# Batch 1's convolution cut by columns instead of by stream, and round 1's side work moved a tile or two

## The chip, the cores and the metric

The kernel runs on one core of one Trainium2 chip. The metric is the device time of one execution in microseconds (us), smaller is better. The profile is of one execution; its span runs from the first to the last instruction of the program on that core. Engines are named as in the profile: PE is TensorE, ACT is ScalarE, DVE is VectorE, POOL is GpSimd, SP is SyncE, which here only issues DMAs.

## The reference

A causal convolution with softmaxed taps per head, then a feed-forward block whose two last matrices follow each other without anything between them:

```python
# x: (8, 3904, 192), weight: (8 heads, 7 taps), group = 192 // 8 = 24 columns per head
w = softmax(weight, axis=-1)
out = einsum('hk,bskhg->bshg', w, windows of 7 rows of zero-padded x)
x = out.reshape(31232, 192)
a, b = x @ w1, x @ w2              # w1, w2: 192 x 1024
h = a * b @ w3                     # w3: 1024 x 1024
return h @ w_out                   # w_out: 1024 x 192
```

## The kernel before, in words

The 31232 tokens are two streams of 15616 (NS = 2): r = 0 is the first half, r = 1 the second. Both go through the kernel side by side in rounds of 512 tokens. `first_product(R)` makes round R's a * b: for each of eight feature tiles ft of 128 it fills a PSUM tile pa (for w1) and a PSUM tile pb (for w2) by six matmuls each, both streams in each; ACT casts pa into asb (line 603), DVE multiplies asb by pb into abT (line 605). `second_product` (line 621) multiplies abT by W_sb, which is w3 @ w_out, made by the kernel itself during the first rounds: `w3_turn` transposes a part of w3 on DVE (line 682), `w3_product` multiplies it by w_out. A dictionary handed to `first_product` names what is issued behind a tile: `{4: f}` calls f when the product of ft 4 has been issued. So the order on each engine is the order in which the program is written out; there is no planner, and each engine works through its queue in that order.

All PSUM tiles (pa, pb, cps, tps, wps, ops) come from one pool of four, handed out in turn: a new tile waits until the reader of the tile four before it is done.

The tokens are convolved in batches of windows of 32 rows, of which 26 come out as results. Batches 0, 1 and 2 have 20 windows per stream, some 520 tokens, one for each of the rounds 0, 1 and 2. POOL issues the loads of x into the tile xb, one per stream for batches 1 and 2 (line 158), stream 0 on partitions 0 to 31, stream 1 on partitions 64 to 95. The convolution is a set of matmuls with 32 x 32 weights (Aband) from xb into a PSUM tile cps; casts bring cps into the tile convo (in bf16, in three blocks k of 64 columns, each with both streams). There are two forms of it:

- `conv(b, c0, wd, evict)` (line 328) takes wd columns from c0 of both streams, 32 matmuls for 96 columns, r innermost. Its casts (line 337, or line 234 where the cast goes through `AV`) follow `segments(c0, wd)`: columns 0 to 95 are 64 columns of block 0 and then 32 of block 1; columns 96 to 191 are 32 of block 1 and then 64 of block 2. With `AV` a segment of 64 columns is cast by ACT and one of 32 by DVE; without `evict` all casts are ACT's.
- `conv_stream(b, r)` (line 357) takes all 192 columns of stream r, also 32 matmuls, two of its casts on ACT and two on DVE (line 364), in that order.

When a batch is in convo, `pe_transposes(b)` (line 401) turns it on PE, 15 transposes into a tile tps, block by block, and copies on ACT (block 0) and DVE (blocks 1 and 2) bring it into xT (line 408), from where the next round's first_product reads it. `store(2, ...)` lets SP write the rows of batch 2 that later rounds need to memory (line 392); `load_taps` then sends the taps through SP (lines 434 and 439).

Where the work around the change stands before: behind round 0's ft 4 and ft 5 the two streams of batch 1, behind ft 6 its transposes; behind round 1's ft 2 and ft 3 the two units of batch 2, behind ft 3 also w3_turn(0), behind ft 5 its transposes and its store.

Of the kernel before, what the change touches and what calls it, by code (L numbers as in the profile page):

```python
# [9 lines left out]
BF16 = mybir.dt.bfloat16  # L10
# [6 lines left out]
def kernel(  # L17
# [10 lines left out]
    nc = tc.nc  # L28

    B, S, D = x.shape  # L30
    H, K = weight.shape
    G = D // H
# [4 lines left out]
    NS = 2  # L37
    TS = B * S // NS
    CH = 512
# [4 lines left out]
    Q = 64  # L44
    NP = D // Q
    C = 32
    ST = C - PAD
    LAG_ROWS = (LAG + 1) * CH
# [43 lines left out]
    work = ctx.enter_context(tc.tile_pool(name="work", bufs=2))  # L92
# [4 lines left out]
    def banks(name):  # L97
        return psum.tile([128, NS, CH], FP32, tag="banks", name=name)
# [13 lines left out]
    def shape_of(b):  # L112
        n = SIZES[b] // 4
        m = n // (1 if b < 3 else 2)
        return n, m, n // m
# [4 lines left out]
    xb_of, zero_rows = {}, {}  # L120

    def group(r, e):
        return slice((2 * r + e) * C, (2 * r + e) * C + C)
# [57 lines left out]
    for r in range(NS):  # L181
        p = group(r, 0).start
# [12 lines left out]
        out=diag, in_=diag, pattern=[[-1, 128 + 8]], compare_op=ALU.is_equal,  # L195
# [11 lines left out]
    for i in range(4):  # L207
        d = diag[i * C:i * C + C, i * C + 2 * i:i * C + 2 * i + C]
        nc.vector.tensor_copy(
            out=cmask[i * C:i * C + C],  # L210
            in_=bass.AP(tensor=d.tensor, offset=d.offset, ap=[d.ap[0], [1, 2], [1, C]]))
# [10 lines left out]
    V, A, P = nc.vector.tensor_copy, nc.scalar.copy, nc.gpsimd.tensor_copy  # L222
# [33 lines left out]
    for i in range(3):  # L256
# [3 lines left out]
        out=share[:, :, 0:K], in0=taps.unsqueeze(1).to_broadcast([H, H, K]), scalar=total,  # L260
        in1=diag[0:H, 0:H].unsqueeze(2).to_broadcast([H, H, K]), op0=ALU.mult, op1=ALU.mult)
    spread = banks("spread")
    for i in range(4):
# [6 lines left out]
        out=wsb, in_=spread[:, 0, 0:2 * H].rearrange("p (h k) -> p h k", h=H)  # L270
# [5 lines left out]
        out=cprod.rearrange("p h k (s two) -> p h k s two", two=2),  # L276
# [6 lines left out]
    p = group(1, 0).start  # L283
    nc.vector.memset(xb_of[0][0][0][p:p + PAD, 0, :], 0.0)
    Aband = const.tile([128, H, C], BF16)
    bps = banks("bps")
    for k in range(2):
# [3 lines left out]
            start=(k == 0), stop=(k == 1))  # L291
    nc.vector.tensor_copy(out=Aband,
                          in_=bps[:, 0, 0:C * H].rearrange("p (h s) -> p h s", s=C))
# [5 lines left out]
    convo_of, left_of = {}, {}  # L299
    wt = {}  # L300

    def segments(c0, n):
        out = []
        while n:
            m = min(n, Q - c0 % Q)
            out.append((c0 // Q, c0 % Q, m))
            c0, n = c0 + m, n - m
        return out

    def conv(b, c0, wd, evict=(nc.scalar.copy,), es=None):  # L310
        n, m, E = shape_of(b)
        es = range(E) if es is None else es
        if b not in convo_of:
            convo_of[b] = work.tile([128, n, NP, NS, Q], BF16, tag="convo", bufs=2,
                                    name="convo")
            left_of[b] = D * E
        convo = convo_of[b]
        cps = {e: banks("cps") for e in es}
        c = c0
        while c < c0 + wd:  # L320
            h = c // G
            c1 = min(h * G + G, c0 + wd)
            for j in range(4):
                xb, s = xb_of[b][j]
                for e in es:
                    for r in range(NS):
                        o = cps[e][j * C:j * C + C, r, 0:m * wd]
                        nc.tensor.matmul(  # L328
                            o.rearrange("p (w g) -> p w g", g=wd)[:, :, c - c0:c1 - c0],
                            Aband[group(r, e), h, :], xb[group(r, e), s:s + m, c:c1],  # L330
                            start=True, stop=True)
            c = c1
        for f, e in zip(evict, es):
            src = cps[e][:, :, 0:m * wd].rearrange("p r (w g) -> p r w g", g=wd)
            o = 0
            for k, lo, c in segments(c0, wd):
                f(out=convo[:, e::E, k, :, lo:lo + c]  # L337
                    .rearrange("p w r g -> p r w g"), in_=src[:, :, :, o:o + c])
                o += c
        left_of[b] -= wd * len(es)  # L340
        if not left_of[b]:
            del xb_of[b]

    def conv_stream(b, r):
        n, m, E = shape_of(b)
        assert E == 1 and 2 * m * D // 2 <= 2 * CH
        if b not in convo_of:
            convo_of[b] = work.tile([128, n, NP, NS, Q], BF16, tag="convo", bufs=2,
                                    name="convo")
            left_of[b] = NS  # L350
        convo = convo_of[b]
        cps, wd = banks("cps"), D // 2
        for h in range(H):
            o = h * G % wd
            for j in range(4):
                xb, s = xb_of[b][j]
                nc.tensor.matmul(  # L357
                    cps[j * C:j * C + C, h * G // wd, 0:m * wd]
                        .rearrange("p (w g) -> p w g", g=wd)[:, :, o:o + G],
                    Aband[group(r, 0), h, :], xb[group(r, 0), s:s + m, h * G:h * G + G],  # L360
                    start=True, stop=True)
        for a, k, lo, o, c, f in ((0, 0, 0, 0, Q, A), (1, 2, 0, C, Q, A),
                                  (0, 1, 0, Q, C, V), (1, 1, C, 0, C, V)):
            f(out=convo[:, :, k, r, lo:lo + c],
              in_=cps[:, a, 0:m * wd].rearrange("p (w g) -> p w g", g=wd)[:, :, o:o + c])
        left_of[b] -= 1
        if not left_of[b]:
            del xb_of[b]

# [211 lines left out]
    def first_product(R, between=None):  # L581
        N = width(R)
        ab = work.tile([128, JT, NS, CH], BF16, tag="abT", bufs=LAG + 1, name="abT")
        abT_of[R] = ab
        per = CH // N if CH % N == 0 else 1
        for f0 in range(0, JT, per):
            pq = []
            for i in range(2):
                p = banks("pa" if i == 0 else "pb")
                pq.append(p)  # L590
                for f in range(per):
                    ft = f0 + f
                    for k in range(NP):
                        for r in range(NS):
                            rs = slice(Q * r, Q * r + Q)
                            nc.tensor.matmul(  # L596
                                p[:, r, f * N:f * N + N],
                                w_of(i, k, r)[rs, ft * 128:(ft + 1) * 128],
                                operand(R, k, rs),
                                start=(k == 0), stop=(k == NP - 1))  # L600
            pa, pb = pq
            asb = work.tile([128, NS, CH], BF16, tag="asb", bufs=3, name="asb")
            nc.scalar.copy(out=asb[:, :, 0:per * N], in_=pa[:, :, 0:per * N])  # L603
            if per == 1:
                nc.vector.tensor_tensor(out=ab[:, f0, :, 0:N], in0=asb[:, :, 0:N],  # L605
                                        in1=pb[:, :, 0:N], op=ALU.mult)
            else:
                i0, i1 = (t.rearrange("p r (f n) -> p r f n", f=per) for t in (asb, pb))
                nc.vector.tensor_tensor(
                    out=ab[:, f0:f0 + per, :, 0:N].rearrange("p f r n -> p r f n"),  # L610
                    in0=i0, in1=i1, op=ALU.mult)
            if between and f0 in between:
                between[f0]()
# [87 lines left out]
    for i in range(4):  # L701
        conv(0, i * 2 * G, 2 * G, evict=((A, V)[i % 2],))
# [33 lines left out]
    starts, chain, begun, room, p = {}, {}, set(), 0, -1  # L736
    for i, cost, f in steps:
# [5 lines left out]
        if i not in begun:  # L743
            begun.add(i)
            starts[p].append(i)
            n = max(p == 0, int(at) // 2 - 1, -(-ends.get(i - 2, 0) // 2))
# [22 lines left out]
    def seq(*fs):  # L769
        def run():  # L770
            for f, *a in fs:
                f(*a)
        return run

    def later_loads():
# [12 lines left out]

    first_product(0, {
        2: later_loads,  # L790
        4: seq((conv_stream, 1, 0)),
        5: seq((conv_stream, 1, 1)),
        6: seq((pe_transposes, 1))})
    first_product(1, {
        2: seq((conv, 2, 0, 96, (AV,))),
        3: seq((conv, 2, 96, 96), (w3_turn, 0)),
        5: seq((pe_transposes, 2), (store, 2, LAG_ROWS // ST))})
    first_product(2, {
        1: seq((load_taps,), (w3_turn, 2)),
        3: seq((w3_product, 0), (w3_product, 2), (w3_turn, 4), (w3_turn, 6),  # L800
# [13 lines left out]
    for p, b, part, n in ((1, 5, 0, 0), (1, 5, 1, 4), (3, 6, 0, 0), (4, 6, 1, 0)):  # L814
        todo = x_jobs(b, part)
        n = n or len(todo)
# [129 lines left out]
```

## Time and profile before

| what | value |
|---|---|
| time, median of 3 runs (lowest to highest) | 511.17 us (510.73 to 512.86) |
| the profiled execution's own time | 510.92 us |
| its span | 509.2 us |
| PE busy | 503.8 us, 99% |
| DVE busy | 446.4 us, 88% |
| ACT busy | 347.2 us, 68% |
| POOL busy | 229.3 us, 45% |

The busy share of PE counts matmuls whose ends are modelled, so it says when PE has work, not how well it is used. Lines are those of the kernel before. A row of the timeline gives start, duration, engine, line, operation, output and input, shape and count; in brackets stands how long the engine was idle just before, and what ended that. In a row with a count above one the duration reaches from the first start to the last end.

### The profile page before, as it was taken

How to read it: one execution, taken by the hardware profiler on the slowest of the kernel's cores; microseconds unless marked ns; L12 is line 12 of the kernel's file. 1: busy time of each engine (PE TensorE's matmuls, PEld its weight loads, DVE VectorE, ACT ScalarE, POOL GpSimd, SP SyncE). 2: the span in 40 equal slices, each digit the busy share in tenths (PEclk: the TensorE clock that was granted, in tenths of full speed). 3: DMA queues.
4: the chain of work that ended last, by engine and by line, in shares of the span. 5: the costliest groups of instructions: out<-in, count | busy, mean ns of one | idle time of the engine just before them, and what ended most of it. 6: DMA issues, size and time to landing. Idle time of an engine off the chain costs nothing.

```text
span 509.2 us, 13681 instructions
## 1 busy us (share of the span) xinstructions
PE 503.8 (99%) x5758; PEld 338.5 (66%) x5758; DVE 446.4 (88%) x402; ACT 347.2 (68%) x386; POOL 229.3 (45%) x303
## 2 busy tenths in 40 slices
PE   8999999999999999999999999999999999999997
PEld 4546864595569557845875596569557855965597
DVE  7898769999999799899989999999899999999930
ACT  6786667836778776477667767763776477457752
POOL 9966101333980597079519902970573067100000
PEclk9999999999999999999999999999999999999999
DMA  9999979999955999963889337975501400230024
GB/s 136 158 162 174 173 152 177 148 163 194 159 60 159 143 158 133 229 79 23 65 219 96 24 106 127 192 110 155 102 1 43 156 4 0 84 106 1 1 63 156
DMA packets 156825, 58.45 MB, mean 115 GB/s; under 512 B 112607, under 2 KB 156763, under 8 KB 156763
## 3 DMA queue, kind: packets, MB, share of 16 engines
q0 software_dynamic: 70560, 16.85, 37.2%
q1 hardware_dynamic: 86043, 40.62, 36.1%
q8 instruction: 45, 0.74, 0.6%
q14 instruction: 17, 0.14, 0.1%
q10 hardware_dynamic: 160, 0.10, 0.1%
HBM read 33.97 MB, written 34.85 MB: 135 GB/s over the span
## 4 chain that ended last, share of the span: by engine, by line
PE 98%; DMA 1%; ACT 0%; POOL 0%; DVE 0%; issue 0%; POOLq 0%
PE ops L621 32%; PE pa L596 31%; PE pb L596 31%; PE cps L328 1%; PE wps L693 1%; DMA xb<-in_x_dram 1%; PE tps L401 0%; PE ops L646 0%; PE tps L416 0%; DVE abT L605 0%; PE cps L357 0%; ACT asb L603 0%; POOL xb L158 0%; ACT convo L337 0%; ACT osb L650 0%
## 5 line engine op out<-in xcount | busy, mean ns | idle before, releaser
L605 DVE TENSOR_TENSOR abT<-asb,pb 128x1024 bf16<-128x1024 bf16 x240 | 292.7, 1221 | 30.4 <-ACT asb L603 14.5
L603 ACT CAST asb<-pa 128x1024 bf16<-128x1024 f32 x244 | 247.0, 1012 | 64.2 <-PE pa L596 64.0
L596 PEld LDWEIGHTS <-wn 64*128 64x128 bf16 x1488 | 138.5, 94 | 79.7 <-issue 1.6
L596 PEld LDWEIGHTS <-ws 64*128 64x128 bf16 x1488 | 129.7, 94 | 70.0 <-issue 1.4
L621 PE MATMUL ops<-W_sb,abT 128*128 128x192 bf16 x1936 | 163.7, 246 | 0.0
L621 PEld LDWEIGHTS <-abT 128*128 128x128 bf16 x1936 | 158.5, 98 | 6.4 <-issue 6.4
L596 PE MATMUL pb<-xT,wn 64*128 64x512 bf16 x408 | 111.2, 376 | 0.0
L596 PE MATMUL pa<-xT,wn 64*128 64x512 bf16 x408 | 110.1, 376 | 0.1
L596 PE MATMUL pa<-xT,ws 64*128 64x512 bf16 x408 | 110.1, 376 | 0.0
L596 PE MATMUL pb<-xT,ws 64*128 64x512 bf16 x408 | 108.5, 376 | 0.0
L626 ACT COPY osb<-ops 128x768 f32<-128x768 f32 (+1 forms) x61 | 48.5, 795 | 84.7 <-PE ops L621 82.3
L876 POOL COPY pace<-abT 1x2 bf16<-1x2 bf16 x57 | 10.9, 192 | 175.5 <-DVE abT L605 155.0
L596 PE MATMUL pb<-side,wn 64*128 64x512 bf16 (+1 forms) x336 | 88.8, 368 | 0.0
L596 PE MATMUL pa<-side,ws 64*128 64x512 bf16 (+1 forms) x336 | 87.3, 369 | 0.0
L596 PE MATMUL pa<-side,wn 64*128 64x512 bf16 (+1 forms) x336 | 87.3, 369 | 0.0
L512 DVE SCALAR_TENSOR_TENSOR acc<-raw,wC,acc 128x1024 f32<-128x1024 bf16 (+2 forms) x70 | 84.6, 1209 | 2.0
L596 PE MATMUL pb<-side,ws 64*128 64x512 bf16 (+1 forms) x336 | 85.7, 368 | 0.0
L539 POOL TENSOR_SCALAR tmp<-acc,wC 128x512 f32<-128x512 bf16 x42 | 65.8, 1566 | 1.2
L559 POOL TENSOR_TENSOR acc<-acc,tmp 128x512 f32<-128x512 f32 x35 | 44.4, 1267 | 2.9
L480 POOL DMA_DIRECT2D rows_c<-in_x_dram x50 | 37.1, 744 | 4.7 <-issue 2.7
L158 POOL DMA_DIRECT2D xb<-in_x_dram x50 | 32.2, 649 | 6.9 <-DMA xb<-in_x_dram 2.2
L512 DVE SCALAR_TENSOR_TENSOR acc<-side,wC,acc 128x1024 f32<-128x1024 bf16 (+1 forms) x20 | 24.3, 1217 | 3.8 <-ACT acc L494 3.2
(76 smaller groups left out, 186.9 us busy)
## 6 DMA issues: line engine op xcount, KB each, us to landing
out_dram<-osb SPq DMA_DIRECT2D x54, 384.0 KB
xb<-in_x_dram POOLq DMA_DIRECT2D x16, 240.0 KB, 7.2
out_dram<-osb SPq DMA_DIRECT2D x12, 192.0 KB
rows_c<-in_x_dram POOLq DMA_DIRECT2D x16, 130.0 KB, 5.6
rows_c<-in_x_dram POOLq DMA_DIRECT2D x12, 128.0 KB, 5.7
rows<-convo SPq DMA_DIRECT2D x6, 240.0 KB
xb<-in_x_dram POOLq DMA_DIRECT2D x6, 228.0 KB, 4.9
w3b<-in_moe_w_dram POOLq DMA_DIRECT2D x4, 256.0 KB, 5.5
```

Source lines behind the costliest of these rows:

```text
L158: nc.gpsimd.dma_start(out=tiles[js[0]][0][group(r, e), s:s + w, :], in_=bass.AP(tensor=x.tensor, offset=(r * TS + t - PAD) * D, ap=[[D, C] ...
L328: nc.tensor.matmul(o.rearrange("p (w g) -> p w g", g=wd)[:, :, c - c0:c1 - c0], Aband[group(r, e), h, :], xb[group(r, e), s:s + m, c:c1], ...
L480: nc.gpsimd.dma_start(out=rows_c[lo:t1, k, r * Q:r * Q + Q], in_=x_rows[r * TS + lo:r * TS + t1, k * Q:k * Q + Q])
L512: nc.vector.scalar_tensor_tensor(out=side_of[p][:, k, o:o + t1 - t0] if last else a, in0=raw[:, HALO + lo - t0 - d:HALO + hi - t0 - d], sc ...
L539: nc.gpsimd.tensor_scalar(out=out, in0=pool_raw[0][:, HALO - d:HALO - d + CH], scalar1=wC[:, k, K - 1 - d:K - d], scalar2=None, op0=ALU.mult)
L559: nc.gpsimd.tensor_tensor(out=a, in0=a, in1=tmp[:, lo - t0:hi - t0], op=ALU.add)
L596: nc.tensor.matmul(p[:, r, f * N:f * N + N], w_of(i, k, r)[rs, ft * 128:(ft + 1) * 128], operand(R, k, rs), start=(k == 0), stop=(k == NP ...
L603: nc.scalar.copy(out=asb[:, :, 0:per * N], in_=pa[:, :, 0:per * N])
L605: nc.vector.tensor_tensor(out=ab[:, f0, :, 0:N], in0=asb[:, :, 0:N], in1=pb[:, :, 0:N], op=ALU.mult)
L621: nc.tensor.matmul(ops[:, g // 2, (g % 2) * D:(g % 2) * D + D], ab[:, jt, r, g * 128:(g + 1) * 128], W_sb[:, jt, :], start=(jt == 0), stop ...
L626: nc.scalar.copy(out=osb.rearrange("p (a g) d -> p a (g d)", g=2), in_=ops[:, 0:ng // 2, 0:2 * D])
L876: P(out=pace, in_=abT_of[R][0:1, ft, 1, 0:2])
```

## The change

`conv_stream` is gone. Batch 1 is convolved by `conv` in two units of 96 columns of both streams, at the same two places, with `AV` for the casts. The first unit of batch 2 is issued behind batch 1's transposes (round 0, ft 6) instead of behind round 1's ft 2; its second unit behind round 1's ft 1 instead of ft 3, and with `AV` instead of ACT alone; w3_turn(0) stays behind ft 3; batch 2's transposes and store go from ft 5 to ft 4. In the changed file every line below `conv` has a number 26 lower.

```diff
-    def conv_stream(b, r):
...
-        for a, k, lo, o, c, f in ((0, 0, 0, 0, Q, A), (1, 2, 0, C, Q, A),
-                                  (0, 1, 0, Q, C, V), (1, 1, C, 0, C, V)):
-            f(out=convo[:, :, k, r, lo:lo + c],
-              in_=cps[:, a, 0:m * wd].rearrange("p (w g) -> p w g", g=wd)[:, :, o:o + c])
...
     first_product(0, {
         2: later_loads,
-        4: seq((conv_stream, 1, 0)),
-        5: seq((conv_stream, 1, 1)),
-        6: seq((pe_transposes, 1))})
+        4: seq((conv, 1, 0, 96, (AV,))),
+        5: seq((conv, 1, 96, 96, (AV,))),
+        6: seq((pe_transposes, 1), (conv, 2, 0, 96, (AV,)))})
     first_product(1, {
-        2: seq((conv, 2, 0, 96, (AV,))),
-        3: seq((conv, 2, 96, 96), (w3_turn, 0)),
-        5: seq((pe_transposes, 2), (store, 2, LAG_ROWS // ST))})
+        1: seq((conv, 2, 96, 96, (AV,))),
+        3: seq((w3_turn, 0)),
+        4: seq((pe_transposes, 2), (store, 2, LAG_ROWS // ST))})
```

More of the change, by code (lines that the diff above doesn't have):

```diff
@@ L340, in conv @@
         left_of[b] -= wd * len(es)
-        if not left_of[b]:
-            del xb_of[b]
-    def conv_stream(b, r):
[L345 to L361, printed above, removed]
-        for a, k, lo, o, c, f in ((0, 0, 0, 0, Q, A), (1, 2, 0, C, Q, A),
-                                  (0, 1, 0, Q, C, V), (1, 1, C, 0, C, V)):
-            f(out=convo[:, :, k, r, lo:lo + c],
-              in_=cps[:, a, 0:m * wd].rearrange("p (w g) -> p w g", g=wd)[:, :, o:o + c])
-        left_of[b] -= 1
         if not left_of[b]:
```

## The prediction

> **What bounds the kernel now.** I read the page first: busy shares, granted clock and the chain that ended last.
>
> ```profile
> span 509.2 us, 13681 instructions
> PE 503.8 (99%) x5758; PEld 338.5 (66%) x5758; DVE 446.4 (88%) x402; ACT 347.2 (68%) x386; POOL 229.3 (45%) x303
> PEclk9999999999999999999999999999999999999999
> PE 98%; DMA 1%; ACT 0%; POOL 0%; DVE 0%; issue 0%; POOLq 0%
> ```
>
> PE is the chain: 98% of the span hangs on it, at full granted clock. From round 0 to the last instruction there is almost no slack on PE, so a microsecond that PE loses or gains early stands in the time. Second, the windows of the two stretches that the diff touches (round 0 is 8.76 to 21.65, round 1 is 21.65 to 34.25):
>
> ```profile
> core 0: us, PE busy (x) PEld busy (x) DVE busy (x) ACT busy (x) POOL busy (x), PEclk, DMA share, GB/s
> 8.76:21.65 12.89, 12.89 (x177) 6.74 (x177) 11.76 (x18) 10.29 (x15) 12.14 (x28) 1.00 1.29 158
> 21.65:34.25 12.60, 12.51 (x177) 6.11 (x175) 11.45 (x13) 10.31 (x13) 7.99 (x15) 1.00 1.34 168
> ```
>
> DVE is busy 91% of both. PE's rhythm leaves the two evicting engines little room, so the third view is PE's timeline:
>
> ```profile
> 15.19 0.38 PE L596 MATMUL pb<-xT,wn 64*128 64x512 bf16 x1
> 15.50 0.60 PE L357 MATMUL cps<-xb,Aband 32*32 32x120 bf16 x32
> 16.03 0.39 PE L596 MATMUL pa<-xT,wn 64*128 64x512 bf16 x1
> ...
> 21.44 0.38 PE L596 MATMUL pb<-xT,wn 64*128 64x512 bf16 x1
> 21.66 0.38 PE L596 MATMUL pa<-xT,wn 64*128 64x512 bf16 x1
> ...
> 22.95 0.38 PE L596 MATMUL pa<-xT,wn 64*128 64x512 bf16 x1
> ...
> 25.63 0.40 PE L328 MATMUL cps<-xb,Aband 32*32 32x120 bf16 x32
> 26.12 0.37 PE L596 MATMUL pa<-xT,wn 64*128 64x512 bf16 x1
> ...
> 27.52 0.40 PE L328 MATMUL cps<-xb,Aband 32*32 32x120 bf16 x32
> 27.86 0.39 PE L596 MATMUL pa<-xT,wn 64*128 64x512 bf16 x1
> ...
> 28.95 0.38 PE L596 MATMUL pb<-xT,wn 64*128 64x512 bf16 x1
> 29.30 0.37 PE L596 MATMUL pa<-xT,wn 64*128 64x512 bf16 x1
> 30.71 1.01 PE L401 MATMUL tps<-diag,convo 128*128 128x128 bf16 x15
> 31.65 0.39 PE L596 MATMUL pa<-xT,wn 64*128 64x512 bf16 x1
> ```
>
> One tile (pa, then pb) takes 22.95 - 21.66 = 1.29, half of it (0.65) for each. A unit of conv_stream delays the next pa by 0.53, a unit of conv by 0.34 (27.52 to 27.86), transposes by 0.94. PE pauses twice here: 25.63 to 26.12 is 0.15 over the 0.34, and 28.95 to 29.30 is 0.14 over the usual 0.21. The chain in order of time names the first pause:
>
> ```profile
> 23.80 1.02 ACT asb L603
> 24.85 1.23 DVE abT L605
> 26.12 0.82 PE pa L596 x6
> ```
>
> The four PSUM tiles are handed out in turn. After one extra tile (cps or tps), the next two pa take buffers that held pb, which only DVE's product frees: PE resumes 0.04 after 26.08.
>
> **The change part by part.** The evicting engines' timelines give the other prices:
>
> ```profile
> 16.89 1.01 ACT L603 CAST asb<-pa 128x1024 bf16<-128x1024 f32 x1
> 18.08 0.75 ACT L364 CAST convo<-cps 128x320 bf16<-128x320 f32 x2 [0.17 <-PE cps L357]
> 18.82 1.01 ACT L603 CAST asb<-pa 128x1024 bf16<-128x1024 f32 x1
> 20.45 0.59 ACT L408 COPY xT<-tps 128x520 bf16<-128x520 bf16 x1 [0.62 <-PE tps L401]
> 26.15 0.69 ACT L234 CAST convo<-cps 128x640 bf16<-128x640 f32 x1
> 28.04 1.02 ACT L337 CAST convo<-cps 128x320 bf16<-128x320 f32 x2
> ...
> 10.82 6.40 DVE L605 TENSOR_TENSOR abT<-asb,pb 128x1024 bf16<-128x1024 bf16 x5 [0.17 <-ACT asb L603]
> 19.08 0.55 DVE L364 CAST convo<-cps 128x160 bf16<-128x160 f32 x2
> 19.87 1.22 DVE L605 TENSOR_TENSOR abT<-asb,pb 128x1024 bf16<-128x1024 bf16 x1 [0.24 <-ACT asb L603]
> 21.08 0.76 DVE L408 COPY xT<-tps 128x520 bf16<-128x520 bf16 x2
> 27.28 0.48 DVE L234 CAST convo<-cps 128x320 bf16<-128x320 f32 x1
> 29.16 1.24 DVE L682 STREAM_TRANSPOSE w3T<-w3b 128x1024 f32<-128x1024 f32 x1
> ```
>
> *Gains.* Two conv_stream units become two conv units with as many matmuls: 2 x (0.53 - 0.34) = -0.39. The pauses of 0.15 and 0.14 stand beside units that move away: -0.29. One unit now follows transposes instead of standing alone between tiles, which saves one break in the rhythm (15.19 to 15.50 is 0.31, the usual 21.44 to 21.66 is 0.22): -0.10. Together -0.78. On ACT and DVE, casts of 2 x 0.75 and 2 x 0.55 become 2 x 0.69 and 2 x 0.48: off the path, nothing by itself.
>
> *The new wait.* A second unit (columns 96 to 191) is evicted in the order of segments(): first 32 columns, on DVE by AV, then 64, on ACT. Both read one cps tile, and the changed program's queues, as built, hold the second reader behind the first:
>
> ```
> DVE L234 TensorCopy convo_422<-cps_475 128x2x5x32 [waits PE_49]
> ACT L234 TensorCopy convo_422<-cps_475 128x2x5x64 [waits DVE_49]
> ```
>
> The same pair stands for batch 2 (cps_634). Before, both casts of batch 2's second unit were ACT's (28.04, 1.02) and in conv_stream ACT came first. Now ACT cannot cast until DVE has done that tile's product and its own cast, and ACT's next asb is queued behind: so is DVE's next product, and PE's buffers.
>
> The Trainium skill, "PSUM — Partial Sum Buffer", section "PSUM bank collisions raise a hardware error", says that ScalarE and VectorE must not read one bank in the same quadrant at once and have to be kept apart by semaphores; so by the page the wait is needed and not an accident. In the trace the nearest case agrees without proving it (ACT's xT copy ends 21.05, DVE's starts 21.08, but DVE was busy until 21.09). With the page the sum is the one below, without it the +0.2 of the first rival.
>
> *First place, round 0, ft 5*, on the clock of before. Batch 1's first unit starts at 15.50; the next pa would start at 15.84 but its buffer waits for the product of ft 3 (one tile ahead of ft 4's, which ends at 10.82 + 6.40 = 17.22) until 15.98 (+0.15). The second unit runs at 17.38. An asb starts 0.86 behind its pa (16.03, 16.89), a product when asb is done: asb of ft 5 16.85 to 17.86; on DVE its product 17.88 to 19.10, the cast to 19.51. ACT: cast 19.54 to 20.23 (before it began at 18.08), asb of ft 6 20.13 to 21.14 (before 18.82). PE: the last transposes need that cast, +0.52 with the buffer of pb; the pa of ft 7 needs asb of ft 6, +0.28; its pb needs the product 21.17 to 22.39, +0.60; +0.03 behind. Sum 1.58.
>
> *Second place, round 1, ft 1.* The same wait: +0.16 for the pa of ft 2; ACT casts at 28.0 where asb could have started at 27.2; the pb of ft 3 takes the buffer of cps, +0.47; the pa of ft 4 waits for asb, +0.26; its pb for the product, +0.61. Sum 1.50.
>
> *Third place, round 1, ft 4 to 6.* w3_turn(0), 1.24 on DVE, loses its companion on PE (a conv unit after ft 3) and now has transposes one tile behind it. Product of ft 3 (31.95), turn (33.1), product of ft 4 (34.2): the pa of ft 6 wants that buffer at 33.9, +0.39 and 0.03 behind. Sum 0.42.
>
> Moved along: store(2) and its two DMAs on SP one tile earlier, with nothing queued behind until the taps; POOL's and SP's order of instructions is unchanged. The convs of batch 1 now need both streams at 15.50:
>
> ```profile
> L158 POOL DMA_DIRECT2D xb<-in_x_dram x4: 682/692/726, 8.2 to 10.3; - x4
> DMA to landing us min/median/max: 7.0/7.3/7.6
> ...
> DMA to landing us min/median/max: 3.8/7.7/9.2
> ```
>
> Four loads issued from 8.2, 0.7 apart: batch 1's second stream at 8.9, batch 2's last at 10.3. The first stream is there at 15.50, the second follows by at most 0.7 if they land as issued: between nothing and +0.7, and I take nothing, since PE would pause 0.15 for a buffer there anyhow. Batch 2 is there at 10.3 + 7.6 = 17.9, its conv now comes at about 20.6: hidden.
>
> *Sum:* 1.58 + 1.50 + 0.42 - 0.78 = +2.7. Profiled execution 510.92 (its span 509.2 and 1.7 around it): 513.6. The median shown, 511.17, lies 0.25 above that execution; so 513.9.
>
> **The rivals.** A difference of 0.5% is 2.56 us here, about what a measurement of this kernel can tell from no change.
>
> 1. *The wait does not bind* (not slower). It decides if ACT's cast goes ahead of DVE's, or the delay of 1.3 in asb fits into PE's buffers. Then the stalls are 0.15, 0.11 at the transposes, 0.13 and 0.06 in round 1, and 0.54 beside w3_turn, 0.99 against gains of 0.78: +0.2, 511.4. For it speaks that ACT is busy only 10.3 of 12.9; against it, that one asb late by more than 0.3 already meets a buffer that PE wants.
> 2. *All gains, no stall:* -0.8, 510.4. For it: casts get shorter on both engines. Against it: the pause at 25.63 is just what a conv of 0.34 costs behind a product.
> 3. *The second stream is late.* At the longest landing, 8.9 + 9.2 = 18.1, the first conv waits 2.6, on top of the rest less what the evictions catch up: about 516. It decides as soon as the landing takes over 6.6. Against it: neighbours took 7.0 to 7.6 though issued later, into a fuller queue.
> 4. *The clock.* If pauses between groups of matmuls cost granted clock, half of it from 19 to 35 would add up to 16 us. The row of PEclk shows full clock through the two pauses of round 1 and the waits before round 0. The Trainium skill, "TensorE: Matmul & The Clock Gate", section "A second HAM failure mode: psum-queue depth-cycling", reports such a loss from cycling PSUM; no slice here shows one.
>
> **How the numbers follow.** The sum as worked out (with 0.4 either way for durations, 0.4 for measuring): 0.75, its own range 513.0 to 514.8; as its middle is barely over the 2.56, I split it 0.47 slower, 0.28 same. Rival 1: 0.12, same. Rival 2: 0.05, 0.03 same and 0.02 faster. Rivals 3 and 4: 0.05 and 0.03, slower. So faster 0.02, same 0.43, slower 0.55. The range for 8 in 10 takes in rival 1: 511.4 to 514.8.
>
> **What would show it.** Each step: two ACT casts at L234 idle behind DVE's convo cast, starting near 19.5 and 28 after waits of over 1 us; then pb of round 0 ft 7 and round 1 ft 4 near 0.6 late; pa of round 1 ft 6 near 0.4 late behind w3_turn; round 2 starting 2.7 later (34.25 before) and nothing changed from there. Wrong it would be if ACT's casts wait under 0.5, if a conv of batch 1 waits for its load, or if rounds behind give the delay back.

## The result and the profile after

| kernel | median | lowest to highest | runs |
|---|---|---|---|
| before | 510.85 us | 510.72 to 512.86 | 6 |
| after | 514.5 us | 513.78 to 516.34 | 6 |

After takes 1.0066 times as long, 95% interval 1.0052 to 1.0081. The six runs of before are the three shown with the kernel before and three more. A ratio here and below is taken over all runs and is not the quotient of two medians (by the medians, after is 3.65 us longer). Predicted were 513.9 us, a ratio of 1.0053 to the 511.17 known then. The profiled execution of after was its longest, 516.34 us; most of what it has over the others is in its first 18 us and not in the change, so I compare stretches that begin at the first convolution of batch 1 and not at the start of the program.

The page of after, with the same rows as shown of before (span, busy time, granted clock, shares of the chain):

```profile
span 514.6 us, 13673 instructions
...
PE 507.8 (99%) x5758; PEld 339.6 (66%) x5758; DVE 446.1 (87%) x401; ACT 346.3 (67%) x383; POOL 229.4 (45%) x303
...
PEclk9999999999999999999999999999999999999999
...
PE 95%; DVE 2%; ACT 1%; DMA 1%; issue 0%; POOL 0%; DVEq 0%; ACTq 0%; POOLq 0%
```

ACT and DVE have no more work than before (346.3 and 446.1 us, before 347.2 and 446.4), but they now own 3% of the chain, where they had nothing. That share says where to look; it is not the loss, which is smaller. The waits of ACT between 17 and 36 us of after (engine and line, released by, us in total, times, longest) name the place:

```profile
ACT convo L234 <- DVE convo L234: 3.4, 2, 1.7
```

Two casts, each 1.7 us behind DVE's cast of the same cps tile. The timelines of ACT and of DVE in after:

```profile
22.00 0.69 ACT L234 CAST convo<-cps 128x640 bf16<-128x640 f32 x1 [1.69 <-DVE convo L234]
22.59 1.02 ACT L577 CAST asb<-pa 128x1024 bf16<-128x1024 f32 x1
...
30.45 0.69 ACT L234 CAST convo<-cps 128x640 bf16<-128x640 f32 x1 [1.69 <-DVE convo L234]
```

```profile
20.34 1.22 DVE L579 TENSOR_TENSOR abT<-asb,pb 128x1024 bf16<-128x1024 bf16 x1 [0.26 <-PE cps L328]
21.48 0.48 DVE L234 CAST convo<-cps 128x320 bf16<-128x320 f32 x1
...
29.93 0.48 DVE L234 CAST convo<-cps 128x320 bf16<-128x320 f32 x1
```

At 20.3 the tile is full and ACT is free, but DVE takes its product first (1.22) and then its cast (0.48); ACT's cast begins when that is done, at 22.00, and the next asb, which stands behind it, at 22.59. PE's timeline of after shows what that costs:

```profile
17.95 0.40 PE L328 MATMUL cps<-xb,Aband 32*32 32x120 bf16 x32
18.43 0.37 PE L570 MATMUL pa<-xT,wn 64*128 64x512 bf16 x1
...
21.61 0.86 PE L375 MATMUL tps<-diag,convo 128*128 128x128 bf16 x10
22.74 0.45 PE L375 MATMUL tps<-diag,convo 128*128 128x128 bf16 x5 [0.27 <-ACT convo L234]
23.13 0.40 PE L328 MATMUL cps<-xb,Aband 32*32 32x120 bf16 x32
23.65 0.37 PE L570 MATMUL pa<-xT,wn 64*128 64x512 bf16 x1
...
24.91 0.37 PE L570 MATMUL pb<-xT,wn 64*128 64x512 bf16 x1 [0.43 <-DVE abT L579]
...
25.59 0.39 PE L570 MATMUL pa<-xT,wn 64*128 64x512 bf16 x1
...
30.12 0.38 PE L570 MATMUL pa<-xT,wn 64*128 64x512 bf16 x1
...
31.19 0.37 PE L570 MATMUL pb<-xT,wn 64*128 64x512 bf16 x1 [0.24 <-ACT convo L234]
...
32.10 0.37 PE L570 MATMUL pa<-xT,wn 64*128 64x512 bf16 x1
...
33.36 0.37 PE L570 MATMUL pb<-xT,wn 64*128 64x512 bf16 x1 [0.43 <-DVE abT L579]
...
36.75 0.37 PE L570 MATMUL pa<-xT,wn 64*128 64x512 bf16 x1 [0.22 <-DVE abT L579]
...
39.38 0.38 PE L570 MATMUL pa<-xT,wn 64*128 64x512 bf16 x1
```

From pa to pb takes 0.65 where nothing is late. Here it is 24.91 - 23.65 = 1.26 in round 0's ft 7, 31.19 - 30.12 = 1.07 in round 1's ft 3 and 33.36 - 32.10 = 1.26 in its ft 4. From the first convolution (17.95) to round 2 (39.38) it is 21.43 us; before, from 15.50 to the row below, it was 18.75.

```profile
34.25 0.38 PE L596 MATMUL pa<-xT,wn 64*128 64x512 bf16 x1
```

The difference is 2.68; the sum of the prediction was 2.7.

### The profile page after: what moved, and what is told of

Same layout as the page of the kernel before. It is cut to its first block, busy times and chain, and to the rows that moved or that the text cites. A ratio compares the mean times of both kernels' runs of the same rounds, so it can differ in the third digit from the quotient of the medians.

```text
span 514.6 us, 13673 instructions
## 1 busy us (share of the span) xinstructions
PE 507.8 (99%) x5758; PEld 339.6 (66%) x5758; DVE 446.1 (87%) x401; ACT 346.3 (67%) x383; POOL 229.4 (45%) x303
## 4 chain that ended last, share of the span: by engine, by line
PE 95%; DVE 2%; ACT 1%; DMA 1%; issue 0%; POOL 0%; DVEq 0%; ACTq 0%; POOLq 0%
PE ops L595 32%; PE pa L570 30%; PE pb L570 30%; DVE abT L579 2%; PE cps L328 1%; PE wps L667 1%; DMA xb<-in_x_dram 1%; ACT asb L577 1%; PE tps L390 0%; PE ops L620 0%; DVE w3T L656 0%; POOL xb L158 0%; ACT osb L600 0%; ACT convo L234 0%; ACT convo L337 0%
## 5 line engine op out<-in xcount | busy, mean ns | idle before, releaser
L570 PE MATMUL pa<-xT,wn 64*128 64x512 bf16 x408 | 111.3, 380 | 0.7 <-DVE abT L579 0.2
L570 PE MATMUL pa<-xT,ws 64*128 64x512 bf16 x408 | 111.3, 380 | 0.0
```

The source lines that it names most:

```text
L570: nc.tensor.matmul(p[:, r, f * N:f * N + N], w_of(i, k, r)[rs, ft * 128:(ft + 1) * 128], operand(R, k, rs), start=(k == 0), stop=(k == NP ...
```

## The experiments

The theory: the second units cost their 1.7 us wait because DVE's cast is first in order, twice; a third, smaller loss is w3_turn without a convolution unit beside it. The main rival: the wait is harmless and something else that the change moved (the shape of the units, the other order) costs the time. "Stretch" below is the time from the first convolution of batch 1 to the first pa of round 2 in the profile of each kernel, 18.75 before. The kernel before took 511.18 us beside e1 to e4 and 511.19 beside e5 to e8.

**e1, e2: ACT's cast first.** The loop of casts in `conv`, in after; e2 does it for batch 1 alone:

```diff
-            o = 0
+            o, segs = 0, []
             for k, lo, c in segments(c0, wd):
+                segs.append((k, lo, c, o))
+                o += c
+            if f is AV and b in (1, 2):          # e2: b == 1
+                segs.sort(key=lambda s: -s[2])
+            for k, lo, c, o in segs:
                 f(out=convo[:, e::E, k, :, lo:lo + c]
...
-                o += c
```

> The changed kernel, but the second units of batches 1 and 2 cast their 64 columns on ACT first and the 32 on DVE behind them; all places stay. If the price is ACT's wait for DVE's cast, the two stalls of about 1.3 us in asb go, and what is left against the kernel before is +0.1 to +0.2 us: 0.15 and 0.16 for the buffers behind the convs, 0.5 us at round 1's ft 6 beside w3_turn, against gains of 0.8. If instead the price lies in the moved places or in both streams going through one unit, nothing changes: +3 to +3.6 us, and pb of round 0's ft 7 is late as before.

> As the run with ACT first, but only for batch 1; batch 2's second unit keeps DVE first. By the wait, only the second place is left: +1.4 us against the kernel before, with asb of round 1's ft 2 idle for over 1 us and no late pb in round 0. If the two places' costs do not add up (the second only late because the first is), it is near 0.

Measured: e1 511.59 us, ratio to before 1.0007 (0.9995 to 1.0018); e2 513.23 us, 1.0033 (1.0023 to 1.0044). PE's timeline of e1, then of e2 (first convolution, round 2):

```profile
15.61 0.74 PE L328 MATMUL cps<-xb,Aband 32*32 32x120 bf16 x32
16.28 0.39 PE L574 MATMUL pa<-xT,wn 64*128 64x512 bf16 x1
...
32.07 0.37 PE L574 MATMUL pa<-xT,wn 64*128 64x512 bf16 x1 [0.33 <-DVE abT L583]
...
34.70 0.38 PE L574 MATMUL pa<-xT,wn 64*128 64x512 bf16 x1
```

```profile
16.21 0.40 PE L328 MATMUL cps<-xb,Aband 32*32 32x120 bf16 x32
...
36.37 0.38 PE L574 MATMUL pa<-xT,wn 64*128 64x512 bf16 x1
```

The stretch is 34.70 - 15.61 = 19.09 in e1 (+0.34) and 36.37 - 16.21 = 20.16 in e2 (+1.41). With the same units at the same places and only the order of two casts turned, 2.3 of the 2.68 are gone; with the order turned in one place, 1.27 are gone. In e1 the 1.7 us wait is no longer among ACT's waits, in e2 it is left once. The two casts of batch 1's second unit in e1, ACT's and then DVE's:

```profile
18.19 0.69 ACT L234 CAST convo<-cps 128x640 bf16<-128x640 f32 x1
```

```profile
19.32 0.48 DVE L234 CAST convo<-cps 128x320 bf16<-128x320 f32 x1
```

The row at 32.07 is the third place: with both casts in order, PE still stops for a product behind w3_turn. The first unit of e1 lasts 0.74 and not 0.40, and its next pa comes 0.67 behind its start, where e6 (below) has 16.04 - 15.56 = 0.48: 0.19 of e1's 0.34 is a wait for the second stream's load. By the medians e1 is +0.41 and e2 +2.05. The latter is more than e2's stretch and the later stop on DVE (+0.28, under e7 and e8) together; the rest is not explained.

**e3: the wait alone, in before.** Nothing else of the change is done:

```diff
-        3: seq((conv, 2, 96, 96), (w3_turn, 0)),
+        3: seq((conv, 2, 96, 96, (AV,)), (w3_turn, 0)),
```

> The kernel before with one edit: batch 2's second unit (behind round 1's ft 3, beside w3_turn) is cast with DVE for its 32 columns first and ACT for its 64 behind, instead of ACT for both. By the wait: +1.0 us, out of a pb 0.5 us late at round 1's ft 5, 0.2 at the transposes and 0.3 at ft 6. If balancing the casts over both engines is what counts, it is no slower than before, or 0.1 us faster.

Measured: 511.79 us, 1.0009 (0.9999 to 1.0019). ACT's waits in e3 between 15 and 36 us, and PE's timeline:

```profile
ACT convo L234 <- DVE convo L234: 1.7, 1, 1.7
```

```profile
15.33 0.60 PE L357 MATMUL cps<-xb,Aband 32*32 32x120 bf16 x32
...
29.13 0.37 PE L596 MATMUL pa<-xT,wn 64*128 64x512 bf16 x1
...
30.25 0.37 PE L596 MATMUL pb<-xT,wn 64*128 64x512 bf16 x1 [0.30 <-ACT convo L234]
...
32.42 0.37 PE L596 MATMUL pa<-xT,wn 64*128 64x512 bf16 x1 [0.26 <-DVE abT L605]
...
35.01 0.38 PE L596 MATMUL pa<-xT,wn 64*128 64x512 bf16 x1
```

The stretch is 19.68, +0.93. A wait of the same 1.7 us costs 0.93 here and not the 1.50 of the second place in after, and that is what was expected of it, step by step: pb of ft 5 is 0.47 late (30.25 - 29.13, less 0.65), the transposes 0.16, pa of ft 6 0.31. In e3 the transposes and w3_turn stand at other tiles behind the wait than in after, so the late asb meets other buffers. By the median it is +0.6, at the edge of what can be told.

**e4: after once more,** unaltered, beside e1 to e3.

> The changed kernel unaltered. The profiled execution of it had TensorE at the lower rate until 13.4 us, where that of the kernel before had full rate from 4.3 us. If that is chance of one execution, this one starts as the kernel before did, its span is 2.7 to 3.0 us over that of before, and round 2 starts 2.7 us later than before. If the change brings it about, the late start is there again and the median stays at +3.6.

Measured: 513.98 us, 1.0045 (1.0028 to 1.0063). The stretch, 15.78 to 37.20 in its profile, is 21.42, +2.67. By the median it is +2.80 us. Its profiled execution took 514.14 us and not 516.34, and the late start of the first one is not there again; the last section shows where those differ.

**e5: the two convolution units of batch 1 alone, in before.**

```diff
-        4: seq((conv_stream, 1, 0)),
-        5: seq((conv_stream, 1, 1)),
+        4: seq((conv, 1, 0, 96, (AV,))),
+        5: seq((conv, 1, 96, 96, (AV,))),
```

> The kernel before with batch 1 convolved in two units of 96 columns at the same two places, cast through AV, DVE first in the second; batch 2, w3_turn and all places stay. By ACT's wait: first conv 0.53 to 0.34, second the same, against 0.15 behind the first, 0.5 at the transposes and 0.8 in round 1's ft 0: +1.1 us. If the wait does its harm only together with batch 2's unit placed right behind it, this is faster than before by 0.3 to 0.4.

Measured: 512.73 us, 1.002 (1.0008 to 1.0032). PE's timeline of e5:

```profile
15.32 0.66 PE L328 MATMUL cps<-xb,Aband 32*32 32x120 bf16 x32
...
20.23 0.45 PE L401 MATMUL tps<-diag,convo 128*128 128x128 bf16 x5 [0.27 <-ACT convo L234]
...
35.23 0.38 PE L596 MATMUL pa<-xT,wn 64*128 64x512 bf16 x1
```

The stretch is 19.91, +1.16: the first place stands without the other two, with the same stop of 0.27 in the transposes as in after. Its first unit lasts 0.66: 0.11 of the 1.16 is again a wait for the second stream's load. By the median e5 is +1.54.

**e6: no wait, and w3_turn with its companion.** On top of e2, the second unit of batch 2 goes back to ACT alone and to one place with w3_turn, and the transposes stay one tile behind w3_turn:

```diff
-        1: seq((conv, 2, 96, 96, (AV,))),
-        3: seq((w3_turn, 0)),
-        4: seq((pe_transposes, 2), (store, 2, LAG_ROWS // ST))})
+        2: seq((conv, 2, 96, 96), (w3_turn, 0)),
+        3: seq((pe_transposes, 2), (store, 2, LAG_ROWS // ST))})
```

> The changed kernel with three edits: batch 1's second unit casts on ACT first; batch 2's second unit is ACT's alone, behind round 1's ft 2, with w3_turn(0) behind it; batch 2's transposes and store behind ft 3. By my steps the two waits and the 0.4 beside w3_turn are gone: round 2 starts 0.4 us earlier than in the kernel before, counted from the first conv. If the third place is not w3_turn but the earlier transposes, pa of round 1's ft 5 stays 0.4 to 0.5 late and it is no faster than before.

Measured: 511.49 us, 0.9995 (0.9983 to 1.0007). PE's timeline of e6:

```profile
15.56 0.40 PE L328 MATMUL cps<-xb,Aband 32*32 32x120 bf16 x32
16.04 0.37 PE L574 MATMUL pa<-xT,wn 64*128 64x512 bf16 x1
...
33.93 0.38 PE L574 MATMUL pa<-xT,wn 64*128 64x512 bf16 x1
...
58.27 0.39 PE L328 MATMUL cps<-xb,Aband 32*32 32x240 bf16 x21 [0.82 <-DMA xb<-in_x_dram]
```

The stretch is 18.37, 0.38 less than before, as expected: with all three places mended, the gains come through. The pa of round 1's ft 5 comes 0.65 behind its pb (29.40, 30.05) and is not late, although the transposes stand one tile behind w3_turn as they do in after; so the third place goes with w3_turn standing without a convolution unit, as far as one run tells that also takes a cast from DVE. But the execution as a whole is not shorter. The last row shows one reason in this execution, a load for batch 4 that came late at 58; its 511.99 us was the longest of its runs, and in the profile of e7 that wait is not there. Another reason is a stop on DVE (next).

**e7, e8: instructions to fill up DVE's count.** In after, DVE idles 0.77 before a product near 316 us, before only 0.49 at the same product; the rows of after, then of before:

```profile
316.71 3.48 DVE L579 TENSOR_TENSOR abT<-asb,pb 128x1024 bf16<-128x1024 bf16 x3 [0.77 <-ACT asb L577]
```

```profile
311.30 3.76 DVE L605 TENSOR_TENSOR abT<-asb,pb 128x1024 bf16<-128x1024 bf16 x3 [0.49 <-ACT asb L603]
```

This is +0.28 for PE, and the only other lasting difference between the two profiles. After has one DVE instruction less than before (401, 402), e6 two less (400), so I tried whether the count sets it: e8 is after with one `nc.vector.memset(one_rows, 1.0)` at the start of `later_loads`, e7 is e6 with two.

> As the run before it, with two small memsets more on DVE in round 0 behind ft 2 (they rewrite a tile that is no longer read), so that DVE has as many instructions ahead of the later rounds as in the kernel before. Four profiles of kernels with one DVE instruction fewer show a DVE stop of 0.74 us near 312 instead of 0.46. If the count of instructions ahead sets it, this one has 0.46 there and is 0.3 us faster than without the fillers; if not, 0.74 stays and it is the same or 0.1 slower.

> The changed kernel with one small memset more on DVE in round 0 behind ft 2, which makes its number of DVE instructions that of the kernel before. If the count sets the stop near 312, it is 0.46 instead of 0.74 and the kernel is 0.3 us faster than the changed one: +2.6 to +2.7 us over before. If not, +2.9 to +3.0.

Measured: e7 511.42 us, 0.9998 (0.9985 to 1.001), stretch 15.71 to 34.09, -0.37; e8 514.0 us, 1.0046 (1.0029 to 1.0064), stretch 15.35 to 37.02, +2.92, of which 0.24 is a wait for a load (below). DVE's timeline of e8, then of e7:

```profile
314.35 2.35 DVE L579 TENSOR_TENSOR abT<-asb,pb 128x1024 bf16<-128x1024 bf16 x2 [0.77 <-ACT asb L577]
```

```profile
405.79 2.35 DVE L583 TENSOR_TENSOR abT<-asb,pb 128x1024 bf16<-128x1024 bf16 x2 [1.09 <-ACT asb L581]
```

At the product near 406 before idles 0.81. PE's first convolution of batch 1 in e8:

```profile
15.35 0.22 PE L328 MATMUL cps<-xb,Aband 32*32 32x120 bf16 x1
15.74 0.40 PE L328 MATMUL cps<-xb,Aband 32*32 32x120 bf16 x31 [0.17 <-DMA xb<-in_x_dram]
16.07 0.39 PE L570 MATMUL pa<-xT,wn 64*128 64x512 bf16 x1
```

Both kernels have before's 402 DVE instructions, and a longer stop stays (0.77 in e8, 1.09 in e7): the count does not set it. In after, e1, e2, e4 and e8 the longer stop comes near 312 to 317, in e5, e6 and e7 near 406, in before and e3 nowhere. What sets it stays open.

## Why the prediction was right

*The new wait* (first and second place). It binds as told: ACT's casts of the second units start behind DVE's cast after waits of 1.69. Rival 1, that it is harmless, is out by e1, where only the order is turned and 2.3 us come back.

*The sizes.* Differences of starts in after, against the terms of the sum:

| term | predicted | in after |
|---|---|---|
| first place: behind the first unit | 0.15 | 0.16 |
| the last transposes | 0.52 | 0.53 |
| pa of round 0 ft 7 (in after, the delay behind the unit at 23.13) | 0.28 | 0.19 |
| pb of round 0 ft 7 | 0.60 | 0.60 |
| the rest of it | 0.03 | 0.07 |
| second place: pa of ft 2 | 0.16 | 0.21 |
| pb of ft 3 | 0.47 | 0.43 |
| pa of ft 4 | 0.26 | 0.27 |
| pb of ft 4 | 0.61 | 0.61 |
| third place: pa of ft 6 and behind it | 0.42 | 0.42 |
| all three | 3.50 | 3.49 |

*The gains* came as told in total (they were not measured one by one): the places sum to 3.49 and the stretch is 2.68 longer, which leaves 0.81 of gains where 0.78 was said. e6 agrees within 0.05: by the measures of the table its PE timeline has 0.15 left behind the first unit, 0.08 at the transposes and 0.15 behind the last unit, and 0.38 - 0.81 is -0.43 where -0.38 was measured. So does e1: the 0.99 of small stalls listed under rival 1, 0.19 for the load, less 0.81, is 0.37; measured was 0.34. Rival 1's working was thus right for a kernel that casts in the other order.

*That the places add up* was assumed and holds from after's side: e2 keeps the second and third place, and e1 only the third. From before's side it holds for the first (e5: 1.58 less the 0.39 of the convolution's form is 1.19, measured 1.16, or 1.05 without the wait for the load). e3 does not test it for the second: there the wait stands at another tile and cost 0.93, as expected for that tile. So 1.50 is the price of that place as it stands in after, not of any such wait.

*What was missing.* "Nothing changed from there" was wrong by the 0.28 on DVE near 316. "I take nothing" for the second stream's load held in after (the 0.40 of the row at 17.95 has no wait in it, but that start was 2 us late) and in e4, and it was luck: by the same two starts the first unit lost 0.19 in e1, 0.11 in e5 and 0.24 in e8. The premise was wrong. The two loads are issued 0.7 apart, but land 1.3 apart in e8 (14.38 and 15.70), e1 (14.55 and 15.90) and e3 (15.09 and 16.40). And the landings of 7.0 to 7.6, given as speaking against a wait, are over the 6.6 that would make one. Rival 3's mechanism is thus real, at a tenth of its price.

*Rival 4, the clock.* Between the stops of after the matmuls last 0.37 to 0.39, so the pauses cost no clock. But its evidence was weak: the row of PEclk shows 9 also where after's matmuls last 0.60 (below), so that row alone could not have shown a loss there. What does settle it is the clock record in after's trace, from which that row is made: it begins at 13.40 (before that there is none, and the row then counts the clock as full) and says full rate without a break to the end.

*The time.* The sum of 2.7 met the stretches of after and e4, 2.68 and 2.67, and left out the 0.28 on DVE. By the medians the change costs 3.65 us in the first comparison, 2.80 in e4 and 2.81 in e8. The first is larger than what the profiles explain, so that 513.9 lies near 514.5 is in part scatter; the other two are what the places and the stop on DVE add up to, within 0.2. The ratios, +0.66%, +0.45% and +0.46%, fit one mechanism of some 2.7 to 3.0 us; by the last two alone, whether it is over 0.5% could not be told.

## What to carry to other kernels

When two engines evict one PSUM tile, write the cast of the engine that is free earlier first: here the second reader was held until the first was done (ACT, free at 20.3, to 22.00), and with it all that was queued behind it. Turning that order was worth 2.3 us in e1. The Trainium skill, "PSUM — Partial Sum Buffer", section "PSUM bank collisions raise a hardware error", says why the two have to be kept apart at all (two engines must not touch one bank in one quadrant together). The trace of after agrees in that ACT was held for 1.69; in e1 DVE was busy with its product until its cast at 19.32 anyhow, so that run does not test it. Count such a wait at the buffers PE asks for next, tile by tile, and not as the length of the wait: here 1.7 us cost between 0.9 and 1.6, depending on what stood beside it.

## What was not expected of the hardware

The two profiled executions of one kernel, after and e4, took 516.34 and 514.14 us. They were apart before the change begins: first convolution of batch 1 at 17.95 and at 15.78. PE's timeline of after, then of e4:

```profile
5.91 0.28 PE L328 MATMUL cps<-xb,Aband 32*32 32x120 bf16 x3
6.64 0.99 PE L328 MATMUL cps<-xb,Aband 32*32 32x120 bf16 x61 [0.45 <-DMA xb<-in_x_dram]
...
9.41 0.60 PE L570 MATMUL pa<-xT,wn 64*128 64x512 bf16 x1
...
13.23 0.47 PE L570 MATMUL pb<-xT,wn 64*128 64x512 bf16 x1
```

```profile
5.91 1.16 PE L328 MATMUL cps<-xb,Aband 32*32 32x120 bf16 x64
...
8.64 0.39 PE L570 MATMUL pa<-xT,wn 64*128 64x512 bf16 x1
```

In after the matmuls of round 0 last 0.60 until about 13.3, in e4 0.39 from the start. In both, PE still ran slowly at 5.9 (three of the first convolution's matmuls take 0.28 in after, 0.23 in before); then PE of after waited 0.45 for the first rows of x, and PE of e4 did not. e2, which also started slowly (its first pa lasts 0.60), had both too: slow at 5.9 and a wait of 0.35. e5 and e8 were slow at 5.9 without that wait, and before, e1, e6 and e7 had the wait after the rate had risen: those six, and e3, began round 0 at 0.39. So in ten profiles a late start goes with a load that arrives while PE is still slow; no run tested it. The clock records of the traces say when the full rate begins: between 4.26 and 6.81 in seven of them (e3 has no record), at 9.99 in e2 and at 13.40 in after, 3.41 later than in e2. The Trainium skill, "TensorE: Matmul & The Clock Gate", section "Part 1: The HAM clock gate (the "warmup" mystery)", has the full clock come after some 3.4 us of sustained work, watched in windows that run free, so that the point varies from run to run; it puts the cost of the ramp under 1% of a typical span. The 3.41 and the 2.2 us (0.4% of the span) fit with it, and a wait that spoils one window would explain e2. It does not explain after by itself: between 6.7 and 10.0 PE of after has no pause over 0.1 us and still stays slow. So the cause of its second delay is open.
